# A maxout kernel on two row halves of TensorE: the upper half's part of a down task is planned 2.8 slots later

## Chip, cores and metric

One core of a Trainium2 chip. The metric is device time in microseconds, the median of the runs of one kernel. All engines named below belong to that one core: TensorE (PE, with its weight loads shown apart as PEld), VectorE (DVE), ScalarE (ACT), GpSimd (POOL) and SyncE (SP).

## What is computed

```python
# x: (8, 4160, 192); weight_gen: (8, 4160, 8 heads, 7 taps)
w = softmax(weight_gen, axis=-1)
out = einsum('bshk,bskhg->bshg', w, windows of 7 rows of x)   # light convolution
t = out.reshape(33280, 192)
h = maximum(maximum(t @ w1, t @ w2), t @ w3)                  # 192 -> 768, three times
result = h @ w_out                                            # 768 -> 192
```

## The kernel before

The 33280 tokens are cut into 65 chunks of 512. For each chunk POOL multiplies the taps (line 246), DVE sums them (line 261), and the result is transposed and split into a high and a low part for TensorE (xa_hi, xa_lo, xb, xc), so that products are exact enough. TensorE then does two kinds of task:

- An **up** task makes a pair of 128x512 blocks of one of the three products, one PSUM bank for each block. A chunk has nine of them.
- A **down** task makes 128 tokens of the result out of h_hi and h_lo of the chunk before, in one PSUM bank. A chunk has four of them, t = 0 to 3, and they stand in the middle of the next chunk's up tasks, after the sixth.

TensorE works as two row halves, 64 rows each, that run at the same time. Each task is done twice: the lower half multiplies rows 0 to 63 of the operands into the bank, and then the upper half multiplies rows 64 to 127 and adds into the same bank. [...] So the last matmul of the lower half's part releases an empty instruction on SP (`state["begun", key]`, line 340), and the first matmul of the upper half's part waits for that instruction. On each half an up task is nine matmuls of 512 columns, and a down task is six pairs of one matmul of 384 columns (wo, h_hi) and one of 192 columns (wo, h_lo).

All matmuls go to one queue, and the order in that queue is planned while the program is built, with two clocks that count slots. A slot is the time of a matmul of 512 columns; 384 columns count 0.86 and 192 count 0.4 (`SLOTS`). `lower` issues the lower half's matmuls one by one and moves clock[0] on. After each one, `advance_upper` issues the upper half's matmuls whose planned start lies before clock[0]. A task's upper part is put into the list `begun` when its lower part is all issued; its planned start is the later of clock[1] and the time noted there ("ready"). Since an up task counts 9 slots, the upper half runs 9 slots behind the lower one. A down task counts 7.56, so the upper half, still busy with an up task, comes to its first down task 1.44 slots after the lower half has planned to end it, and so for t = 1 to 3.

The order of DVE, ACT, POOL and SP follows from ticks (22 for each chunk), and from the place where an upper part is complete: then `maximum` (DVE and ACT read the bank, lines 376 and 378) or `add` (lines 410 and 411) is issued or put on a later tick. The PSUM pool has 8 banks that are used in turn.

Of the kernel before, what the change touches and what calls it, by code (L numbers as in the profile page):

```python
# [98 lines left out]
def lightconv_maxout_kernel(  # L99
# [322 lines left out]

    clock = [0.0, 0.0]
    begun = collections.deque()

    def advance_upper(limit):
        while begun:
            ready, work = begun[0]
            if max(clock[1], ready) >= limit:
                return  # L430
            slots = next(work, None)
            if slots is None:
                begun.popleft()
            else:
                clock[1] = max(clock[1], ready) + slots

    def lower(task, first=0, last=None):

        f, *args = task
        if first == 0:  # L440
            state["lower"] = f(*args, 0)
        for slots in itertools.islice(state["lower"], None if last is None else last - first):
            clock[0] += slots
            advance_upper(clock[0])
        if last is None:
            begun.append((clock[0], f(*args, 1)))


    words = [w.bitcast(U32) for w in (w1, w2, w3, w_out)]
# [117 lines left out]
    NC = len(chunks)  # L567
# [66 lines left out]
    for c in range(NC + 1):  # L634
        for tick in range(TICKS):
# [3 lines left out]
            if 2 * DOWN_AT <= tick < 2 * DOWN_AT + TC:  # L639
                if c == 1:  # L640
                    for j in range(NJ):
                        finish(f"d{j}")
                if 0 < c < NC:
                    lower((down, c - 1, tick - 2 * DOWN_AT, range(NJ)))
                continue
# [6 lines left out]
            if c == NC:  # L652


                if tick < TC:
                    lower((down, c - 1, tick, range(NJ - 2)))
                elif tick >= 2 * DOWN_AT + TC and tick < 2 * DOWN_AT + 2 * TC:
                    t = tick - 2 * DOWN_AT - TC
                    if t == 0:
                        advance_upper(float("inf"))  # L660
                    lower((down, c - 1, t, range(NJ - 2, NJ)))
            elif odd == 0:
                lower((up, (c, *divmod(k, 3))), 0, 4)
            else:
                lower((up, (c, *divmod(k, 3))), 4)
# [37 lines left out]
```

## Time and profile before

| | us |
|---|---|
| median of 3 runs | 1708.07 |
| the runs | 1707.27 to 1709.53 |
| span of the profiled execution | 1706.2 |
| PE busy in it | 1666.9 (98%) |
| POOL busy | 1427.5 (84%) |
| ACT busy | 1147.3 (67%) |
| DVE busy | 1128.4 (66%) |

The time of the profiled execution outside its span isn't listed; the median of the runs lies 1.9 us above the span. A matmul's end in the trace is modelled, and matmuls overlap, so that "98% busy" doesn't mean that the array can't be quicker. What can be read are starts: the distance from one matmul's start to the next of its half.

### The profile page before, as it was taken

What the parts mean: (1) busy time and instruction counts of PE and PEld (TensorE: products, weight loads), DVE (VectorE), ACT (ScalarE), POOL (GpSimd) and SP (SyncE); (2) the same over time, 40 slices, a digit from 0 to 9 for tenths busy, and PEclk for the clock granted to TensorE, in tenths of its full rate; (3) what the DMA queues carried; (4) which work ended last, traced back from release to release, by engine and by line L of the source; (5) the groups of instructions that cost most, each with busy time, mean ns of one, the idle gap of its engine ahead of it and who ended that gap; (6) DMA issues with size and microseconds to landing.
All of it is one profiled execution on the core that took longest, in us unless ns stands there. A gap on an engine that the chain in (4) does not pass through costs nothing.

```text
span 1706.2 us, 42191 instructions
## 1 busy us (share of the span) xinstructions
PE 1666.9 (98%) x16794; PEld 1643.2 (96%) x16794; DVE 1128.4 (66%) x1552; ACT 1147.3 (67%) x2896; POOL 1427.5 (84%) x844
## 2 busy tenths in 40 slices
PE   3899999999999999999999999999999999999999
PEld 2599999999999999999999999999999999999999
DVE  7966766666666666666666676666666666666653
ACT  5657667766766766766766766766676676676672
POOL 6888888888888898888888898988889888888872
PEclk9999999999999999999999999999999999999999
DMA  7010110101010110101010110101011010101000
GB/s 235 1 70 10 70 53 27 70 20 69 12 70 20 60 70 21 60 21 69 11 70 29 52 69 20 61 20 70 11 69 64 26 61 20 70 11 46 20 11 29
DMA packets 20422, 79.51 MB, mean 47 GB/s; under 512 B 2320, under 2 KB 5128, under 8 KB 17536
## 3 DMA queue, kind: packets, MB, share of 16 engines
q1 hardware_dynamic: 20104, 76.54, 11.8%
q8 instruction: 131, 2.15, 0.5%
q14 instruction: 67, 0.55, 0.1%
q10 hardware_dynamic: 120, 0.28, 0.1%
HBM read 51.25 MB, written 25.56 MB: 45 GB/s over the span
## 4 chain that ended last, share of the span: by engine, by line
PE 95%; DVE 3%; DMA 1%; SPq 0%; issue 0%; POOL 0%; ACT 0%; DVEq 0%
PE ph L329 95%; DVE acc L261 1%; DVE m L378 0%; DMA wt<-in_weight_gen_dram 0%; DVE ph L481 0%; DVE ph L486 0%; DVE e L493 0%; DVE ph L479 0%; DVE ph L492 0%; DMA xt<-in_x_dram 0%; SPq L527 0%; SPq L519 0%; DVE red L215 0%; POOL wt L217 0%; DVE xb L309 0%
## 5 line engine op out<-in xcount | busy, mean ns | idle before, releaser
L246 POOL TENSOR_TENSOR r<-xt,wt 128x1344 f32<-128x1344 f32 x260 | 721.9, 2815 | 0.8 <-DMA xt<-in_x_dram 0.5
L378 DVE TENSOR_TENSOR m<-ph,m 128x512 f32<-128x512 f32 x780 | 522.9, 685 | 216.3 <-PE ph L329 119.5
L385 POOL TENSOR_TENSOR h_lo<-m,h_hi 128x512 fp32r<-128x512 f32 x390 | 502.6, 1299 | 169.1 <-ACT h_hi L381 164.3
L329 PE MATMUL ph<-xa_hi,wa_hi 64*128 64x512 f32 x2340 | 627.0, 390 | 8.6 <-ACT xa_hi L300 2.8
L329 PE MATMUL ph<-xa_lo,wa_hi 64*128 64x512 f32 x2340 | 623.1, 387 | 1.0 <-DVE xa_lo L304 1.0
L329 PE MATMUL ph<-xa_hi,wa_lo 64*128 64x512 f32 x2340 | 621.9, 387 | 0.6 <-POOL wa_lo L496 0.6
L329 PE MATMUL ph<-xb,wb_hi 64*128 64x512 f32 x2340 | 622.4, 387 | 0.0
L329 PE MATMUL ph<-wo,h_hi 64*128 64x384 f32 x3120 | 594.9, 358 | 0.0
L329 PE MATMUL ph<-wo,h_lo 64*128 64x192 f32 x3120 | 554.6, 249 | 0.0
L381 ACT CAST h_hi<-m 128x512 fp32r<-128x512 f32 x390 | 241.9, 621 | 399.1 <-DVE m L378 396.0
L329 PEld LDWEIGHTS ph<-wo,h_hi 64*128 64x128 f32 x3120 | 486.6, 184 | 5.6 <-issue 0.4
L329 PEld LDWEIGHTS ph<-wo,h_lo 64*128 64x128 f32 x3120 | 485.1, 187 | 0.1
L261 DVE TENSOR_REDUCE acc<-r 128x192 f32<-128x1344 f32 x260 | 401.8, 1547 | 110.0 <-POOL r L246 110.0
L290 ACT COPY room<-room 32x128 f32<-32x128 f32 x1488 | 440.7, 296 | 26.0 <-DVE room L284 7.8
L329 PE MATMUL ph<-xc,wb_lo 64*128 64x512 f32 x1170 | 453.0, 387 | 0.0
L329 PEld LDWEIGHTS ph<-xa_hi,wa_hi 64*128 64x128 f32 x2340 | 364.8, 185 | 15.4 <-ACT xa_hi L300 3.3
L329 PEld LDWEIGHTS ph<-xa_hi,wa_lo 64*128 64x128 f32 x2340 | 357.3, 185 | 3.0 <-POOL wa_lo L496 1.0
L329 PEld LDWEIGHTS ph<-xa_lo,wa_hi 64*128 64x128 f32 x2340 | 357.4, 185 | 2.9 <-DVE xa_lo L304 1.5
L329 PEld LDWEIGHTS ph<-xb,wb_hi 64*128 64x128 f32 x2340 | 357.6, 185 | 2.1
L376 ACT COPY m<-ph 128x512 f32<-128x512 f32 x390 | 221.5, 585 | 53.7 <-PE ph L329 47.7
L411 DVE TENSOR_TENSOR o<-ph,ob 128x192 f32<-128x192 f32 x260 | 86.8, 353 | 235.7 <-ACT ob L410 235.5
L329 PEld LDWEIGHTS ph<-xc,wb_lo 64*128 64x128 f32 x1170 | 216.0, 185 | 1.4 <-POOL wb_lo L496 0.2
(54 smaller groups left out, 702.8 us busy)
## 6 DMA issues: line engine op xcount, KB each, us to landing
xt<-in_x_dram SPq DMA_DIRECT2D x20, 1728.0 KB, 7.1
out_dram<-o SPq DMA_DIRECT2D x64, 384.0 KB, 2.3
wt<-in_weight_gen_dram SPq DMA_DIRECT2D x21, 336.0 KB, 3.1
h_hi<-in_moe_w_dram SPq DMA_DIRECT2D x6, 256.0 KB, 4.5
xt<-in_x_dram SPq DMA_DIRECT2D x1, 1536.0 KB, 9.7
h_lo<-in_moe_w_dram SPq DMA_DIRECT2D x6, 192.0 KB, 5.0
room<-in_moe_w_out_dram SPq DMA_DIRECT2D x1, 1152.0 KB, 8.1
xt<-in_x_dram SPq DMA_DIRECT2D x1, 960.0 KB, 5.9
```

The lines of the kernel that those rows point to most:

```text
L246: nc.gpsimd.tensor_tensor(r.rearrange("p (h g) k -> p k h g", g=G), xt[:, la + t : la + t + K].rearrange("p k (h g) -> p k h g", g=G), wt[ ...
L261: nc.vector.tensor_reduce(state["acc", c][:, t], r, axis=AX.X, op=ALU.add)
L290: pin(nc.scalar.copy(to[:, :, p : p + 32], blocks[p : p + 32, :, f : f + 32]))
L329: ins = nc.tensor.matmul(ph[:, :n], w[h], v[h], start=begins and half == 0 and q == 0, stop=ends and half == 1 and q == len(terms) - 1,)
L376: pin(nc.scalar.copy(m[:, :N], ph[:, :N]))
L378: pin(nc.vector.tensor_tensor(m[:, :N], ph[:, :N], m[:, :N], op=ALU.max))
L381: later(1, lambda: pin(nc.scalar.copy(hi, m[:, :N])))
L385: nc.gpsimd.tensor_tensor(lo, m[:, :N], hi.bitcast(F32), op=ALU.subtract)
L411: pin(nc.vector.tensor_tensor(o[:, t], po[:, :D], ob, op=ALU.add))
```

## The change

```diff
     clock = [0.0, 0.0]
     begun = collections.deque()
+    SETTLE = 2.8
...
         if last is None:
-            begun.append((clock[0], f(*args, 1)))
+            settle = SETTLE if f is down and args[0] < NC - 1 else 0.0
+            begun.append((clock[0] + settle, f(*args, 1)))
```

The upper part of a down task is noted as ready 2.8 slots after the lower part's planned end, for all chunks but the last. The matmuls themselves, their operands and what waits for what stay as they were; only the order in TensorE's queue is another. At the first down task of the program the upper half's plan skips 1.36 slots (2.8 less the 1.44 that it was behind anyway), and since it never catches up, it is 10.36 slots behind the lower half from there on, in all chunks.

The orders of ACT, POOL and SP come out the same as before, and that of DVE too except for two neighbours that change places once, near the start.

TensorE, the end of the lower half's part of down task t = 0 in the middle of the program, before. ph_10665 is the bank of t = 0, ph_10700 that of t = 1; ph_10649 is a bank of the up task that the upper half still works on. The third row from the end is the upper half's first matmul into the bank of t = 0, which waits for SP.

```order
L329 MATMUL ph_10649<-xc_10288,wb_lo_83 128x512
L329 MATMUL ph_10665<-wo_84,h_lo_10105 128x192 [waits Pool_49]
L329 MATMUL ph_10700<-wo_84,h_hi_10104 128x384 [waits DVE_49]
L329 MATMUL ph_10649<-xa_hi_10285,wa_lo_81 128x512
L329 MATMUL ph_10700<-wo_84,h_lo_10105 128x192
L329 MATMUL ph_10700<-wo_84,h_hi_10104 128x384
L329 MATMUL ph_10665<-wo_84,h_hi_10104 128x384 [waits SP_sequencer_49]
L329 MATMUL ph_10700<-wo_84,h_lo_10105 128x192
L329 MATMUL ph_10665<-wo_84,h_lo_10105 128x192
```

The same place with the change, where the numbers of the tiles are others: ph_10664 is the bank of t = 0, ph_10699 that of t = 1, ph_10647 the up task's.

```order
L329 MATMUL ph_10647<-xa_lo_10285,wa_hi_80 128x512
L329 MATMUL ph_10664<-wo_84,h_lo_10107 128x192 [waits Pool_49]
L329 MATMUL ph_10647<-xb_10286,wb_hi_82 128x512
L329 MATMUL ph_10699<-wo_84,h_hi_10106 128x384 [waits DVE_49]
L329 MATMUL ph_10647<-xc_10287,wb_lo_83 128x512
L329 MATMUL ph_10699<-wo_84,h_lo_10107 128x192
L329 MATMUL ph_10699<-wo_84,h_hi_10106 128x384
L329 MATMUL ph_10647<-xa_hi_10284,wa_lo_81 128x512
L329 MATMUL ph_10699<-wo_84,h_lo_10107 128x192
L329 MATMUL ph_10699<-wo_84,h_hi_10106 128x384
L329 MATMUL ph_10664<-wo_84,h_hi_10106 128x384 [waits SP_sequencer_49]
L329 MATMUL ph_10699<-wo_84,h_lo_10107 128x192
```

The waiting matmul stood behind three matmuls of the lower half's t = 1 (h_hi, h_lo, h_hi); now it stands behind five (h_hi, h_lo, h_hi, h_lo, h_hi). The upper half's matmul that stands last ahead of the lower part's end is the second one of its block of five (xa_lo), where it was the fourth (xc).

TensorE, the place where the upper half comes back from the down tasks to an up task, before. ph_10764 is the bank of t = 3, ph_10795 the upper half's up task, and ph_10813 and ph_10826 are the lower half's.

```order
L329 MATMUL ph_10813<-xa_hi_10285,wa_lo_81 128x512
L329 MATMUL ph_10764<-wo_84,h_lo_10105 128x192
L329 MATMUL ph_10826<-xa_hi_10285,wa_hi_80 128x512 [waits DVE_49]
L329 MATMUL ph_10795<-xa_hi_10285,wa_hi_80 128x512 [waits SP_sequencer_49]
L329 MATMUL ph_10826<-xa_lo_10286,wa_hi_80 128x512
L329 MATMUL ph_10795<-xa_lo_10286,wa_hi_80 128x512
```

And with the change, where the bank of t = 3 is ph_10762, the upper half's up task is ph_10793, and the lower half's new up task is ph_10824.

```order
L329 MATMUL ph_10824<-xa_hi_10284,wa_hi_80 128x512 [waits DVE_49]
L329 MATMUL ph_10762<-wo_84,h_hi_10106 128x384
L329 MATMUL ph_10762<-wo_84,h_lo_10107 128x192
L329 MATMUL ph_10824<-xa_lo_10285,wa_hi_80 128x512
L329 MATMUL ph_10793<-xa_hi_10284,wa_hi_80 128x512 [waits SP_sequencer_49]
L329 MATMUL ph_10824<-xb_10286,wb_hi_82 128x512
L329 MATMUL ph_10793<-xa_lo_10285,wa_hi_80 128x512
```

The upper half's first matmul of the up task stood beside the lower half's first of the next one; now it stands beside the lower half's second. From there on the halves alternate as they did, one matmul further apart.

## Prediction

> **What bounds the kernel.** I read the page first: PE's share of the span, then the chain of work that ended last.
>
> ```profile
> PE 1666.9 (98%) x16794; PEld 1643.2 (96%) x16794; DVE 1128.4 (66%) x1552; ACT 1147.3 (67%) x2896; POOL 1427.5 (84%) x844
> ...
> PE ph L329 95%; DVE acc L261 1%; DVE m L378 0%; DMA wt<-in_weight_gen_dram 0%; DVE ph L481 0%; DVE ph L486 0%; DVE e L493 0%; DVE ph L479 0%; DVE ph L492 0%; DMA xt<-in_x_dram 0%; SPq L527 0%; SPq L519 0%; DVE red L215 0%; POOL wt L217 0%; DVE xb L309 0%
> ...
> L329 PEld LDWEIGHTS ph<-wo,h_hi 64*128 64x128 f32 x3120 | 486.6, 184 | 5.6 <-issue 0.4
> ```
>
> 95% of the chain is line 329, the matmuls, so time can only come from how closely these follow each other. One group of weight loads has idle time ahead of it that no engine of the profile explains: 5.6 us before the loads for wo, h_hi.
>
> Next, the mean clock and the busy times over three neighbouring chunks, cut where the lower half starts its first down task.
>
> ```profile
> 639.62:664.98 25.36, 25.36 (x261) 25.28 (x259) 16.11 (x22) 17.82 (x46) 21.58 (x13) 1.00 0.05 17
> 664.98:690.34 25.36, 25.36 (x261) 25.28 (x259) 16.34 (x22) 16.60 (x44) 20.97 (x13) 1.00 0.05 17
> 690.34:715.70 25.36, 25.36 (x261) 25.28 (x259) 17.85 (x24) 17.87 (x46) 23.04 (x15) 1.00 0.26 100
> ```
>
> A chunk lasts 25.36 us at full clock (1.00), though POOL's work differs (20.97 to 23.04); PE repeats itself, and PEld has a hole of 0.08 us in each chunk. The timeline of PE around one such place shows where a chunk's time goes. Two rows that start close together are the two halves.
>
> ```profile
> 621.21 0.42 PE L329 MATMUL ph<-xa_hi,wa_hi 64*128 64x512 f32 x1
> ...
> 621.47 0.39 PE L329 MATMUL ph<-xa_lo,wa_hi 64*128 64x512 f32 x1
> ...
> 622.17 0.39 PE L329 MATMUL ph<-xa_hi,wa_lo 64*128 64x512 f32 x1
> ...
> 623.30 0.44 PE L329 MATMUL ph<-xa_hi,wa_hi 64*128 64x512 f32 x2
> ...
> 639.62 0.33 PE L329 MATMUL ph<-wo,h_hi 64*128 64x384 f32 x1
> ...
> 639.79 0.25 PE L329 MATMUL ph<-wo,h_lo 64*128 64x192 f32 x1
> ...
> 640.80 0.39 PE L329 MATMUL ph<-xa_lo,wa_hi 64*128 64x512 f32 x1
> ...
> 641.03 0.39 PE L329 MATMUL ph<-xb,wb_hi 64*128 64x512 f32 x1
> 641.21 0.25 PE L329 MATMUL ph<-wo,h_lo 64*128 64x192 f32 x1
> 641.26 0.39 PE L329 MATMUL ph<-xc,wb_lo 64*128 64x512 f32 x1
> 641.30 0.36 PE L329 MATMUL ph<-wo,h_hi 64*128 64x384 f32 x1
> 641.48 0.39 PE L329 MATMUL ph<-xa_hi,wa_lo 64*128 64x512 f32 x1
> 641.50 0.25 PE L329 MATMUL ph<-wo,h_lo 64*128 64x192 f32 x1
> 641.59 0.62 PE L329 MATMUL ph<-wo,h_hi 64*128 64x384 f32 x2
> 641.78 0.34 PE L329 MATMUL ph<-wo,h_lo 64*128 64x192 f32 x1
> 641.97 0.35 PE L329 MATMUL ph<-wo,h_hi 64*128 64x384 f32 x1
> 642.05 0.25 PE L329 MATMUL ph<-wo,h_lo 64*128 64x192 f32 x1
> ```
>
> At 639.62 the lower half starts t = 0. It ends it with the matmul of 641.21, goes on with t = 1 at 641.30, and the upper half, which had its up task's last matmul at 641.48, should follow with its own t = 0. The row of 641.59 holds two matmuls: the lower half's second h_hi of t = 1, and the upper half's first of t = 0. When the latter could start is told by the weight loads, from two looks at PEld.
>
> ```profile
> 641.50 0.18 PEld L329 LDWEIGHTS ph<-wo,h_hi 64*128 64x128 f32 x1
> ```
> ```profile
> 641.77 0.18 PEld L329 LDWEIGHTS ph<-wo,h_hi 64*128 64x128 f32 x1
> 641.77 0.29 PEld L329 LDWEIGHTS ph<-wo,h_lo 64*128 64x128 f32 x2
> 641.88 0.19 PEld L329 LDWEIGHTS ph<-wo,h_hi 64*128 64x128 f32 x1
> ```
>
> The load of 641.50 is the lower half's. The next one in the queue is the upper half's, which carries the wait for SP, and it starts at 641.77, 0.27 us later. The lower half's own load for the matmul of 641.78 stands behind it and starts in the same hundredth. So one wait holds both halves. SP's instruction runs in between:
>
> ```profile
> L340 SPq EVENT_SEMAPHORE  x2: 17/17/17, 641.7 to 643.4; - x2
> ```
>
> **The price of the wait, worked out twice.** First from the chunk. From 623.30 to 639.62 the lower half does eight up tasks, 72 matmuls, in 16.32 us: 0.2267 each. From 639.79 to 641.21 it does five pairs in 1.42 us: 0.284 a pair. A chunk has 81 up matmuls and 24 pairs on each half: 81 x 0.2267 + 24 x 0.2845 = 18.36 + 6.83 = 25.19. The chunk takes 25.36, so 0.17 us of it is neither.
>
> Second from the upper half. Its last up matmul starts at 641.48; 0.227 later the first h_hi is due. Behind an up matmul the h_lo follows its h_hi by 639.79 - 639.62 = 0.17, so the upper half's first h_lo is due at 641.88. It starts at 642.05: 0.17 late. The two agree, so nearly all that a chunk loses is lost at this one place. The lower half loses less here: from 641.59 to 641.97 two h_hi are 0.38 apart where a pair takes 0.284, about 0.1. The rest it loses further on, since the order in the queue ties it to the upper half.
>
> **The change, part by part.** The new constant removes no instruction and adds none. Its one effect is the order of 16770 matmuls.
>
> (a) The wait at t = 0. In the new order the waiting load stands behind the lower half's third h_hi of t = 1, not the second. That third h_hi's load can go when the h_lo before it starts, at 641.78, and the upper half is now 1.36 slots x 0.2267 = 0.31 us later: its last up matmul moves from 641.48 to 641.79, and its first down load isn't wanted before that. The release came at 641.77. Even if it came no earlier, nothing would wait. It should come earlier. The lower half's last matmul ends at 641.21 + 0.25 = 641.46, and yet the load starts 0.31 after that; the upper half's xc matmul, which stands ahead of it in the queue, ends at 641.26 + 0.39 = 641.65, 0.12 before the load. With the change the upper matmul ahead of it is xa_lo, begun at 640.80 + 0.31 = 641.11 and ended at 641.50, so the release falls to about 641.62. That leaves 0.17 us to spare.
>
> [...]
>
> So 0.17 x 64 chunk boundaries = 10.9 us is what can be won at most. The least would be nothing, if the wait were only moved. I look for what stays. After the change the lower half is the one that may still lose: beside the upper half's down tasks its up matmuls follow each other more slowly, 622.17 - 621.47 = 0.70 for three, 0.02 more than 3 x 0.2267, in each chunk. This isn't the wait's doing, so I keep 0.02 and take 0.15: 64 x 0.15 = 9.6 us. I take the value near the upper end because 0.17 came out of two independent readings.
>
> (b) t = 1 to 3. The upper half begins these 2.8 slots after the lower half's end instead of 1.44, so their waits only get 0.31 us more room. They cost nothing now (the 0.17 is used up by t = 0), so nothing is won.
>
> (c) The end of the program. The upper half is 1.36 slots further behind when the lower half is done, and runs that much longer alone: + 0.31 us, once. The chain shows that nothing covers it:
>
> ```profile
> 1689.99 12.84 PE ph L329 x104
> 1702.83 0.02 issue
> ```
>
> (d) The other engines. Every bank is complete 0.31 us later, so DVE's and ACT's reads of it are, and the bank comes free later. What hides this are the 8 banks, and the queues, which wait for PE rather than PE for them:
>
> ```profile
> DVE m L378 <- PE ph L329: 119.5, 190, 2.3
> ```
> ```profile
> PE ph L329 <- DVE m L378: 2.6, 4, 1.6
> ```
>
> PE's four waits for DVE's m, 2.6 us in all, are too few to be one in each chunk. If that cover were gone, the price would be up to 0.31 us at each place. The SP queue's order is unchanged, so the stores and loads behind it keep their places; POOL, the next busiest engine, has the same order and 25.36 us for at most 23.04 us of work. A chunk of 25.21 still holds that.
>
> The sum, against the profiled span: 1706.2 - 9.6 + 0.3 = 1696.9. The median of the runs lies 1.9 above the span, and nothing in the change touches what lies there: 1708.1 - 9.3 = **1698.8 us**, 0.5% faster. A difference under 0.2%, 3.4 us, couldn't be told from no change here.
>
> **Rivals.**
>
> *No gain, 1708.* The wait could be worth nothing: if TensorE let the lower half's weight loads pass the one that waits, the halves would drift apart by themselves until nothing waited, and an order that plans for it would bring nothing. Against it: in the trace the lower half's load starts in the same hundredth as the held one, not before, and the chunk repeats to 25.36 three times with its hole in PEld, so no drift has cured it. [...] Or the release moves along with the upper half, and the wait with it; the 0.17 to spare speaks against that. Chance 0.08 for both.
>
> *Half the gain, 1703.* With the halves at another distance, their loads may meet in a worse way in the queue: of the upper half's 0.17 the lower half's own 0.1 could come back, at a place where one half's load stands ahead of its time. 64 x 0.08 = 5.1, less 0.3: 1703.3. For it: the halves are tied by the order at all places, and back in the up tasks the upper one now stands 0.36 slots off the lower one's rhythm, where it was in step. Against it: a load holds up the next by 0.11 us (641.77 to 641.88), and an up matmul gives 0.227 for the two halves' loads. Chance 0.13.
>
> *Slower, 1718.* The later completion of banks makes the lower half's first load of an up task wait for DVE, once a chunk. The point from which it decides is where DVE's read of a bank ends less than 0.31 us before the bank is wanted; then up to 0.31 x 64 = 19.8 us come on top of the gain: 1698.8 + 19.8 = 1718.6. DVE has long pieces of work in its queue (line 261), which speaks for it; that it waits 119.5 us for PE and PE 2.6 us for it speaks against. Chance 0.04.
>
> **How the numbers follow.** The forecast has 0.75. Its own range goes from the full 0.17 without a rest (1708.1 - 10.9 + 0.3 = 1697.5, less 1.0 for the spread of the runs) to 0.11 a chunk (1701.4). To leave out no more than 2 in 10 the whole range reaches to the half gain: 1696.5 to 1703.4. Faster by over 0.2%: 0.75 and nearly all of the half gain, 0.87; within 0.2%: 0.09; slower: 0.04.
>
> **What the profile after would show.** A chunk of 25.19 to 25.23 us; PEld's idle time ahead of the loads for wo, h_hi down from 5.6 us to under 1; the upper half's first down load without a hole before it; PE still the chain, with the end 0.3 us longer after the last lower matmul. I'd be wrong if the chunk kept 25.36 with the hole at another place, or if waits of PE for DVE m showed some 64 times.

## The result, and the profile after

| | us |
|---|---|
| before, median of 5 runs | 1707.34 (1707.17 to 1709.53) |
| with the change, median of 5 runs | 1698.55 (1697.86 to 1699.39) |
| ratio, with its 95% interval | 0.9944 (0.9933 to 0.9956) |
| profiled execution: its time, its span | 1699.39, 1697.6 |
| predicted | 1698.8 (1696.5 to 1703.4) |

The page after, its first line and the group that had unexplained idle time:

```profile
PE 1657.2 (98%) x16794; PEld 1466.1 (86%) x16794; DVE 1124.6 (66%) x1552; ACT 1145.8 (67%) x2896; POOL 1426.2 (84%) x844
...
L329 PEld LDWEIGHTS ph<-wo,h_hi 64*128 64x128 f32 x3120 | 398.4, 184 | 2.9 <-issue 0.4
```

Busy times over two neighbouring chunks, cut again where the lower half starts its first down task:

```profile
637.97:663.16 25.19, 25.19 (x262) 22.42 (x259) 15.89 (x21) 18.17 (x46) 21.98 (x14) 1.00 0.05 17
663.16:688.34 25.18, 25.18 (x260) 22.42 (x258) 16.32 (x22) 16.74 (x43) 20.79 (x13) 1.00 0.05 18
```

A chunk takes 25.19 us where it took 25.36, the sum of the matmuls' own distances as the prediction had it. The place itself, in the timeline of PE and of PEld:

```profile
637.97 0.33 PE L329 MATMUL ph<-wo,h_hi 64*128 64x384 f32 x1
637.97 0.39 PE L329 MATMUL ph<-xa_hi,wa_lo 64*128 64x512 f32 x1
...
639.56 0.25 PE L329 MATMUL ph<-wo,h_lo 64*128 64x192 f32 x1
...
640.01 0.39 PE L329 MATMUL ph<-xa_hi,wa_lo 64*128 64x512 f32 x1
640.13 0.25 PE L329 MATMUL ph<-wo,h_lo 64*128 64x192 f32 x1
640.22 0.36 PE L329 MATMUL ph<-wo,h_hi 64*128 64x384 f32 x2
640.41 0.25 PE L329 MATMUL ph<-wo,h_lo 64*128 64x192 f32 x2
640.50 0.36 PE L329 MATMUL ph<-wo,h_hi 64*128 64x384 f32 x2
640.70 0.25 PE L329 MATMUL ph<-wo,h_lo 64*128 64x192 f32 x2
```
```profile
639.96 0.19 PEld L329 LDWEIGHTS ph<-wo,h_lo 64*128 64x128 f32 x1
640.01 0.30 PEld L329 LDWEIGHTS ph<-wo,h_hi 64*128 64x128 f32 x2
640.24 0.19 PEld L329 LDWEIGHTS ph<-wo,h_lo 64*128 64x128 f32 x2
```

The upper half's last up matmul starts at 640.01 and its first h_hi at 640.24 (the second one in the row of 640.22, in step with the lower half's third), 0.23 later: on time. The row of 640.01 holds two loads. Here is the first one alone, and SP's instruction:

```profile
640.01 0.18 PEld L329 LDWEIGHTS ph<-wo,h_hi 64*128 64x128 f32 x1
```
```profile
L340 SPq EVENT_SEMAPHORE  x1: 17/17/17, 639.8 to 639.8; - x1
```

The first one is the upper half's; in the trace it is the load that carries the wait for SP. It starts as soon as the upper half's matmul before it has started (640.01), so nothing holds it: SP's instruction had ended at 639.86 by the trace. The second one, the lower half's, starts with that half's h_lo at 640.13, although its matmul stands ahead of the other's in the queue. So here the load of one half, which nothing held, went 0.12 us ahead of one of the other half that stands before it in the queue. From there on both halves run in step, a pair every 0.29 (640.41 to 640.70).

Where the 8.65 us between the two profiled spans (1706.23 and 1697.57 before rounding) are: these four rows are the lower half's first down matmul at the sixth chunk boundary (chunk 5) and at the last one (chunk 63), first two of before, then two of after, from the timelines of PE of the two kernels.

```profile
208.50 0.33 PE L329 MATMUL ph<-wo,h_hi 64*128 64x384 f32 x1
...
1679.38 0.33 PE L329 MATMUL ph<-wo,h_hi 64*128 64x384 f32 x1
```
```profile
209.80 0.33 PE L329 MATMUL ph<-wo,h_hi 64*128 64x384 f32 x1
...
1670.62 0.33 PE L329 MATMUL ph<-wo,h_hi 64*128 64x384 f32 x1
```

Between them lie 58 chunks: 1470.88 us before, 1460.82 after, 10.06 less, or 0.173 a chunk. The opening is 1.30 longer in this execution, and what follows the last of these rows is 0.10 longer (26.85 against 26.95). 10.06 - 1.30 - 0.10 = 8.66.

### The profile page after: what moved, and what is told of

The parts are those of the page before. It is cut to its first block, busy times and chain, and to the rows that moved or that the text cites. A ratio compares the mean times of both kernels' runs of the same rounds, so it can differ in the third digit from the quotient of the medians.

```text
span 1697.6 us, 42191 instructions
## 1 busy us (share of the span) xinstructions
PE 1657.2 (98%) x16794; PEld 1466.1 (86%) x16794; DVE 1124.6 (66%) x1552; ACT 1145.8 (67%) x2896; POOL 1426.2 (84%) x844
## 3 DMA queue, kind: packets, MB, share of 16 engines
q8 instruction: 131, 2.15, 0.5%
## 4 chain that ended last, share of the span: by engine, by line
PE 94%; DVE 3%; ACT 1%; DMA 1%; POOL 1%; SPq 0%; issue 0%; DVEq 0%
PE ph L329 94%; DVE acc L261 1%; DVE m L378 0%; DMA wt<-in_weight_gen_dram 0%; DVE ph L483 0%; POOL r L246 0%; DVE ph L488 0%; DVE e L495 0%; DVE ph L481 0%; DVE ph L494 0%; DMA xt<-in_x_dram 0%; SPq L529 0%; ACT room L290 0%; SPq L521 0%; POOL h_lo L385 0%
## 5 line engine op out<-in xcount | busy, mean ns | idle before, releaser
L329 PE MATMUL ph<-wo,h_lo 64*128 64x192 f32 x3120 | 522.3, 247 | 0.0
L329 PEld LDWEIGHTS ph<-wo,h_lo 64*128 64x128 f32 x3120 | 398.8, 188 | 2.5
L329 PEld LDWEIGHTS ph<-wo,h_hi 64*128 64x128 f32 x3120 | 398.4, 184 | 2.9 <-issue 0.4
L329 PEld LDWEIGHTS ph<-xa_hi,wa_hi 64*128 64x128 f32 x2340 | 338.7, 185 | 53.9 <-DVE m L378 3.9
L329 PEld LDWEIGHTS ph<-xa_hi,wa_lo 64*128 64x128 f32 x2340 | 338.4, 185 | 42.0 <-POOL wa_lo L498 1.5
L329 PEld LDWEIGHTS ph<-xa_lo,wa_hi 64*128 64x128 f32 x2340 | 338.7, 185 | 38.7 <-DVE xa_lo L304 1.5
L329 PEld LDWEIGHTS ph<-xb,wb_hi 64*128 64x128 f32 x2340 | 338.7, 185 | 38.4 <-ACT xb L308 0.3
```

Of the source, the lines that this page charges most:

```text
L329: ins = nc.tensor.matmul(ph[:, :n], w[h], v[h], start=begins and half == 0 and q == 0, stop=ends and half == 1 and q == len(terms) - 1,)
```

## The experiments

The runs with a DMA or with more empty instructions aside, each kernel differs from the changed one only in the number or in the condition beside it; times are medians, and ratios are against the kernel before, run beside it on the same chip.

**One skip for half of the program.** The condition is `args[0] == 32`.

> The 2.8 slots are applied to the down tasks of chunk 32 alone. Theory A (one skip of 1.36 slots holds for the rest of the program): chunks of 25.36 us up to there and 25.19 after it, 32 x 0.173 = 5.5 us gained, 0.3 lost at the end: 1702.1. Rival (each down task needs its own settling time): one chunk gains, 1707.

Measured: 1703.06, ratio 0.9968 (0.9956 to 0.9979). Two neighbouring chunks ahead of chunk 32 and two behind it, the lower half's first down matmul in the timeline of PE:

```profile
842.37 0.33 PE L329 MATMUL ph<-wo,h_hi 64*128 64x384 f32 x1
```
```profile
867.72 0.33 PE L329 MATMUL ph<-wo,h_hi 64*128 64x384 f32 x1
```
```profile
918.26 0.33 PE L329 MATMUL ph<-wo,h_hi 64*128 64x384 f32 x1
```
```profile
943.45 0.33 PE L329 MATMUL ph<-wo,h_hi 64*128 64x384 f32 x1
```

25.35 us before the skip, 25.19 after it. One shift holds for the rest of the program: the 1708.61 - 1703.06 = 5.55 us gained against the kernel beside it are about 32 x 0.173.

**A later release, with the order of before and with the new one.** A DMA of four bytes is issued by SP ahead of the empty instruction, for t = 0 alone (`spare` is a small tile of its own, set to zero once; the result isn't touched):

```diff
             if q == len(terms) - 1 and not (ends and half == 1):
+                if isinstance(key[0], int) and key[1] == 0:
+                    pin(after(nc.sync.dma_start(out=spare[:1, 1:2], in_=spare[:1, :1]), ins))
                 state["begun", key] = pin(after(nc.sync.nop(), ins))
```

> The order of before (constant 0), with a real delay in the release for t = 0: SP issues a DMA of four bytes between two spare elements before the empty instruction. An issue of SP's takes 0.33 to 0.34 us in the trace of before, so with the waits around it d should be 0.35 to 0.45 us. Theory A (the wait at t = 0 is on the path in each chunk): 25.36 + d a chunk, that is 25.71 to 25.81, and 1708 + 64 d: 1730 to 1737. Rival (the wait isn't what limits): 25.36, 1708.

> The same DMA in the order with 2.8 slots. There the load is issued 0.23 us after its release, and in the order of before 0.28 us of waiting cost 0.17 a chunk, so some 0.11 more is swallowed by the load's lead over its matmul. Theory A: d - 0.34 a chunk is left, 25.19 to 25.30, 1698.5 to 1706. Rival (the new order is quicker for another reason than this wait): d shows in full as it does in the order of before, 25.54 to 25.64, 1721 to 1727.

Measured: 1750.85 in the order of before, ratio 1.0244 (1.0229 to 1.026), and 1721.89 in the new one, ratio 1.0078 (1.0061 to 1.0094). The issue took longer than I had read off the larger DMAs (the line's instructions with the order of before; minimum, median and maximum in ns):

```profile
L343 SPq DMA_DIRECT2D spare<-spare x67: 543/591/685, 84.2 to 1742.8; - x67
```

So both numbers are beyond what was expected, while the difference between them, 29 us, isn't far from theory A's 31 (the rival's was 9 to 10). The 1721.89 lies in the range given beside the rival, 1721 to 1727, but that range was for a delay of 0.35 to 0.45; with what the delay costs in the order of before, 0.67 a chunk (below), the rival would have given 1698.5 + 64 x 0.67 = 1741. The timeline of PE with the order of before, and then with 2.8 slots, one chunk each:

```profile
706.71 0.33 PE L331 MATMUL ph<-wo,h_hi 64*128 64x384 f32 x1
```
```profile
732.74 0.33 PE L331 MATMUL ph<-wo,h_hi 64*128 64x384 f32 x1
```
```profile
694.68 0.33 PE L331 MATMUL ph<-wo,h_hi 64*128 64x384 f32 x1
```
```profile
720.35 0.33 PE L331 MATMUL ph<-wo,h_hi 64*128 64x384 f32 x1
```

The chunk of the new order shown here, 25.67, is one of the longer ones. By the mean of the last 58 chunks: 26.03 instead of 25.36 in the order of before, 0.67 more, so the delay passes into every chunk nearly in full; 25.57 instead of 25.19 in the new order, 0.38 more. Counted from the lower half's first down matmul, SP's instruction came 0.70 and 0.75 us later than without the DMA. The new order swallowed 0.75 - 0.38 = 0.37 of it; expected was 0.34.

The sum agrees with the expectation, its terms don't. The 0.23 us between release and load were read from the lower half's load of 640.13. The load that waits starts 0.16 us after SP's instruction ends, and in the trace of before, where it does wait at t = 0, 0.04 after it, so the room is 0.12. Under the delay the upper half falls back by another 0.17 (its last up matmul starts 2.21 us behind the lower half's first down matmul, without the DMA 2.04), and of the 0.46 by which the load is then late, 0.08 doesn't reach the chunk. Together that is the 0.37. That the wait lies on the path, and that the new order swallows a part of the delay where the old one doesn't, is shown by this pair.

**The same with a still later place.** The constant is 4.06, with the DMA:

> The delayed release once more, in the order with 4.06 slots, where the upper half's first down matmul starts 2.53 us after the lower half's, against 2.27 with 2.8. With 2.8 the delay left 0.37 us a chunk. Theory A (what counts is the time between the release and the load that waits for it, and a slot planned more swallows as much as it lasts): 0.37 - 0.26 = 0.11 left, 25.30 a chunk, 1698.3 + 64 x 0.11 = 1705.3. Rival (the later place does nothing for this wait): 0.37 left, 1722.

Measured: 1709.16, ratio 1.0007 (0.9997 to 1.0016). A chunk takes 25.34 on the mean, 0.15 over its 25.19, where 0.11 was expected. Of the 0.26 later place 0.38 - 0.15 = 0.23 counted. The release itself came 0.07 us later than with 2.8 and the DMA; another of the upper half's matmuls stands last ahead of the lower half's end there, which would explain it. Of the distance to the expected time the profiled executions show 1.29 us ahead of the sixth chunk boundary (210.67 against 209.38 us with 4.06 alone) and 0.43 behind the last one (27.61 against 27.18).

**Empty instructions as a delay.** Four more empty instructions on SP in the same place.

> The order of before (the constant is 0), and SP's release for t = 0 made later: four more empty instructions on SP stand between the end of the lower half's part and the upper half's first matmul, for t = 0 alone. Call the delay that they add d (to be read off the trace, some 0.07 to 0.25 us). Theory A (this wait is on the path, in each chunk): a chunk takes 25.36 + d, the kernel 1707.3 + 64 d, for d = 0.1 that is 1713.7. Rival (the wait isn't what limits): unchanged, 1707.3.

> The same later release in the order with 2.8 slots. There the load is issued 0.23 us after the release in the trace, so theory A has it swallow d as long as d is under about 0.23: 25.19 a chunk, 1698.5; if d is larger, the excess shows, 64 times. Rival: the delay costs the same as in the order of before, 64 d.

Measured: 1708.13, ratio 1.0004 (0.9995 to 1.0012), and 1698.71, ratio 0.9947 (0.9934 to 0.9961). The 0.07 to 0.25 us expected for d were the author's estimate; no run shows them. The trace has one SP instruction of 17 ns at t = 0 as before (1371 of line 340 and 67 of line 343 together, where before has 1438 of line 340), so no delay arose and the pair tells nothing of the wait. It is a repeat of both kernels, and of use as that (below).

**Only the matmul ahead of the lower half's end is another one.** The constant is 1.6.

> The constant is 1.6 instead of 2.8, so that the upper half falls back by 0.16 slots only. Its first down matmul keeps its place in the queue (behind the lower half's second h_hi of t = 1, as before the change), but the upper half's xc matmul now stands behind the lower half's last matmul of t = 0 instead of ahead of it. Theory A (the wait is as long as it is because the release waits for every matmul ahead in the queue to end, and the xc matmul was one of them): the release comes some 0.15 to 0.2 us earlier, nearly the whole wait goes, a chunk takes 25.19 to 25.22 us and the kernel 1698.5, at most 1700. Theory B (the gain comes from the distance, in proportion to the slots that the upper half falls back): 0.16 of 1.36 slots, a gain of 1.0 us, 1706.3.

Measured: 1707.43, ratio 0.9988 (0.9979 to 0.9997); of eleven runs ten took 1705.98 to 1708.45 and one 1700.8. The expectation of theory A failed. B's gain of 1.0 us is close to the 1.2 against the kernel beside it (1708.61), but a gain in proportion to the slots doesn't go with the plateau below, and it says nothing of the quick run. The first profile was of that run; a second one followed:

> The constant 1.6 once more, for a second profile. Its one profiled execution was at 1700.8 us with chunks of 25.21 and 25.25, while ten others took 1706.0 to 1708.5. Theory A: in those the first down load waits in each chunk again, with a hole ahead of it, and a chunk takes 25.32 to 25.36. Rival: the chunks are as quick as in the first profile, and the time is lost elsewhere, in the opening or at the end.

Measured: 1708.13, the usual speed. The timeline of PE and PEld around its place:

```profile
692.67 0.39 PE L329 MATMUL ph<-xb,wb_hi 64*128 64x512 f32 x1
692.75 0.25 PE L329 MATMUL ph<-wo,h_lo 64*128 64x192 f32 x1
...
693.12 0.39 PE L329 MATMUL ph<-xa_hi,wa_lo 64*128 64x512 f32 x1
...
693.35 0.41 PE L329 MATMUL ph<-wo,h_hi 64*128 64x384 f32 x2
```
```profile
693.19 0.18 PEld L329 LDWEIGHTS ph<-wo,h_hi 64*128 64x128 f32 x1
693.19 0.18 PEld L329 LDWEIGHTS ph<-wo,h_lo 64*128 64x128 f32 x1
```

The lower half's t = 0 ends at 692.75 + 0.25 = 693.00, the upper half's xb, now the last one ahead of it in the queue, at 692.67 + 0.39 = 693.06, and the load that waits goes at 693.19: 0.13 after xb, where it was 0.12 after xc in the profile before. So in both orders the release comes behind the other half's matmul ahead in the queue, and the wait at t = 0 is nearly gone: the load is 0.06 late where it was 0.28 late before, and the upper half's first h_hi starts at 693.35, 0.23 after its last up matmul. Yet the chunk takes 25.34. The time is lost in what follows, as this stretch of the same timeline shows:

```profile
694.11 0.31 PE L329 MATMUL ph<-wo,h_lo 64*128 64x192 f32 x2
...
696.14 0.31 PE L329 MATMUL ph<-wo,h_lo 64*128 64x192 f32 x2
```

Seven pairs of the upper half in 2.03: 0.290 each, not 0.2845. It keeps this pace through all its down tasks in the trace; over the 24 pairs of a chunk that is 0.13. The prediction's second rival had feared something of the kind, for loads that meet in the queue. The trace doesn't show that the upper half's loads wait: they start as soon after the matmul before them as with 2.8, and it is the h_lo matmuls that start some 6 ns later behind their loads (0.179 against 0.173 us on the mean). Why is not shown. What sets which of the two speeds an execution falls into stays open too; at the first down matmul the halves' distance in the quick run was 0.03 to 0.05 us smaller than in the slower one.

**More room.** Constants of 2.2, 3.2, 4.06 and 11.8.

> The constant 2.2: the upper half's first down matmul stands one matmul earlier than with 2.8 (behind the lower half's second h_lo of t = 1, not its third h_hi), and in the down tasks the halves' matmuls alternate in another pattern (h_hi of one beside h_lo of the other). Theory A (only the release's margin counts; here still over 0.1 us): 25.19 a chunk, 1698.4. Theory C (the pattern of the weight loads counts, as 1.6 showed, where pairs of the upper half took 0.290 instead of 0.2845): 25.22 to 25.34, 1700 to 1707.5.

> The constant 3.2: the same place in the lower half's row as with 2.8 or one later, the release's margin larger by 0.4 x 0.227 = 0.09 us, and the alternating pattern of 1.7 to 2.0. Theory A: 25.19 a chunk, 1698.6. Theory C: 25.22 to 25.34, 1700 to 1707.5.

> The constant is 4.06, one pair of down matmuls (1.26 slots) more than 2.8. Theory A: nothing waits already at 2.8, so a chunk stays at 25.19 and only the end is longer by 1.26 x 0.227 = 0.29 us: 1698.9. Theory C (what counts is how the two halves' matmuls lie beside each other): another offset gives another chunk, 25.25 to 25.36, 1702 to 1707.

> The constant is 11.8: nine slots, a whole up task, more than 2.8, so that the upper half is 19.36 slots behind. Theory A: chunks of 25.19 and an end longer by 9 x 0.227 = 2.0 us: 1700.6. The slower rival of the prediction (banks come free too late): waits of PE for DVE or ACT in each chunk, up to 2 us each, 1710 or more.

Measured: 1699.3, ratio 0.994 (0.9922 to 0.9958), for 2.2; 1698.15, ratio 0.9939 (0.9921 to 0.9957), for 3.2; 1698.3, ratio 0.9939 (0.9925 to 0.9953), for 4.06. All have chunks of 25.19; with 2.2 a few of 25.29 stand among them. Their patterns in the queue differ and their times don't; of what theory C feared only the 1.6 shows anything. With 2.2 there is no room left: the load that waits is held in every chunk, by 0.05 us in the trace, and that little doesn't show in the chunk. From 2.2 to 4.06 there is a plateau, and no version beats the change by more than the measurement tells.

With 11.8 the kernel takes 1788.28, ratio 1.0464 (1.045 to 1.0478). The longest waits of TensorE's loads (us in total, times, longest):

```profile
PEld ph L329 <- ACT m L376: 70.5, 123, 1.3
PEld ph L329 <- DVE m L378: 21.1, 26, 3.1
```

Behind 19.36 slots the banks aren't free in time: TensorE's loads wait 70.5 us for ACT's and 21.1 us for DVE's reads, and nearly all chunks take 26.0 to 27.5 us. The prediction's slower rival is real, only further off, and more for ACT than for DVE.

## Why the prediction was right

- **The wait at t = 0 and its price.** Right: 0.17 a chunk by two readings, and 0.173 was won in each of 58 chunks. `half` shows it appear at the skip; the pair with the DMA shows that a delay of this wait passes into the chunk.
- **The 0.02 that the lower half would keep.** Wrong. The three matmuls 0.02 too slow beside the upper half's down tasks were read as the lower half's own; they went with the wait (the same three take 0.68 after, by the trace), and the chunk came to the full 25.19. This made the predicted gain 64 x 0.02 = 1.3 us too small.
- **64 boundaries.** Wrong by five. The first five chunks won nothing: in the repeat of the new order `hop_after`, the lower half starts the down tasks there at 208.65 us, against 208.50 in the profile before. That is 5 x 0.17 = 0.9 us less gain, and it hid the mistake before. With both set right the terms give 59 x 0.173 less 0.27 at the end (0.10, and the last boundary's 0.17 that is in it), 9.9 us; the spans of the two repeats, `hop_before` and `hop_after`, differ by 9.84 (1706.28 and 1696.43). The medians of the result differ by 8.8, and 9.3 were forecast from a time of before that was 0.7 above the median measured with the result. That 1698.8 and 1698.55 lie so near is in part luck.
- **How far the upper half falls back.** 0.31 us by the plan; in the trace its last up matmul moved from 1.86 to 2.04 us behind the lower half's first down matmul, 0.18, and its first down matmul from 2.15 to 2.27, 0.12. Why it fell back by less than the plan's 0.31 is not shown; that the plan's distance is a limit, within which the upper half goes as early as it can, is the author's reading. The room for the release came out at 0.12 us, not 0.17: the release fell earlier by 0.22, not 0.15, since the lower half's own last matmul now ends after xa_lo (639.81 and 639.72 by the trace), but the load is wanted earlier too, and it goes ahead of the lower half's third h_hi load, behind which the prediction had it. The end, put at 0.31, grew by 0.10, in which the last boundary's own gain of 0.17 is counted.
- **PEld's idle time ahead of wo, h_hi.** 2.9, not under 1. In the trace the hole of 0.08 us ahead of the load that waits is gone; the 2.9 is another one, 0.04 in each chunk, ahead of the lower half's first down load. PEld's share fell from 96% to 86%: in the up tasks the halves' loads now start in twos (two at 632.53, two at 632.76) and leave holes, in all 38 to 54 us ahead of each of the four groups of 2340 loads where it was 2 to 15, and the chunk takes its 25.19 all the same. As a sign of the wait the number was badly chosen, since it adds up all loads of the group.
- **The rivals.** No gain: excluded by the chunk, 25.19 against 25.36. Half the gain: it didn't come at 2.8; 1.6 loses time in the pairs of down matmuls, though not in a way that shows the loads meeting. Slower: not at 2.8, and shown at 11.8. The sentence that t = 1 to 3 cost nothing holds for the two orders compared; for others it isn't shown.

## What to carry to other kernels

Where two streams share a queue as here, one that waits for the other can stop both (before, both halves' loads start at 641.77, 0.27 us after the load ahead of them); give it a planned distance that covers the release's way (here from the modelled end of the other half's matmul ahead in the queue by way of SP to the load, 0.12 to 0.13 us), and one shift at the start is enough, as it was in `half` (25.35 us a chunk before it, 25.19 after it). Take the distance from the middle of a plateau, by trying values on both sides: at 1.6 slots the wait was nearly gone and the time wasn't won (1707.43 us), at 2.2 to 4.06 it was (1698.15 to 1699.3), and at 11.8 the loads waited for the banks (1788.28). Add up what one period of the steady part must take from its rows, and compare it with what it takes: the difference, here 0.17 us of 25.36, is what a better order can win as long as it leaves those distances as they are.

## What the runs showed of the hardware

In two of these orders the release that depends on the lower half's matmul came only after the upper half's matmul that stands ahead of it in the queue: the load followed that one's modelled end by 0.12 us before and by 0.13 in `s16b`, though the lower half's own matmul had ended 0.31 and 0.19 us before the load. It wasn't SP that was slow: its instruction took 17 ns, and before, the semaphore that TensorE counts up and SP waits for has no increment in the trace between 640.75 and 641.66, while the lower half's last matmul ends at 641.46 by the model.

In the opening of these two executions TensorE ran at half clock once, for 3.4 us, and not at the same place. After, and then in the profile before (the granted clock is the number behind the five engines):

```profile
77.00:82.00 5.00, 4.33 (x22) 3.13 (x24) 4.70 (x8) 1.48 (x5) 5.00 (x6) 0.66 0.00 0
```
```profile
77.66:81.07 3.41, 3.40 (x16) 2.76 (x18) 3.21 (x5) 0.81 (x3) 3.41 (x6) 0.50 0.00 0
```
```profile
50.00:60.00 10.00, 7.79 (x49) 5.34 (x47) 9.76 (x20) 8.16 (x19) 4.35 (x5) 0.83 0.00 1
...
77.00:82.00 5.00, 4.01 (x36) 3.13 (x37) 4.79 (x8) 1.67 (x5) 5.00 (x6) 1.00 0.00 0
```

Before, it fell between 50 and 60 us, where PE is idle for a fifth of the time anyway; in the profiled execution after, between 77 and 82, where 22 matmuls started instead of 36. In `hop_after`, with the same order, it fell between 50 and 60 again, and the first down task started at 80.73 us instead of 81.86. So 1.1 us of the 1.30 that the opening seemed to lose go with the place of this stretch and not with the order. The fourteen profiles of the case bear this out: in five such a stretch lies between 77 and 83 us, and the first down task starts at 81.67 to 82.31; in the other nine none lies there, and it starts at 80.20 to 81.24.

A DMA of four bytes between two spots of SBUF kept SP for 0.54 to 0.69 us (`delay_before` and `delay_after`, line 343), longer than a store of 384 KB to DRAM, whose issue took 0.33 to 0.35 (before, line 419).
